# Block 0 by a fixed plan, four loads with places of their own, and tile loads issued from another queue

## The chip, the core and the metric

The kernel runs on one core of a Trainium2 chip. The metric is the device time in microseconds (us) of one execution. A core has five engines with an instruction queue each: TensorE (PE in the profile, with its weight loads as PEld), VectorE (DVE), ScalarE (ACT), GpSimd (POOL) and SyncE (SP). SP computes nothing here; it issues transfers (DMA), which ACT and POOL can do too. Each queue is worked off in order, so an instruction that waits holds up all that stand behind it on its engine.

## The reference

What is computed is an attention without softmax, with a norm, followed by a two-layer network with a leaky relu:

```python
kv = np.einsum('bhsd,bhse->bhde', k, v)          # 8 batches, 8 heads, 576 tokens, 64 wide
out = np.einsum('bhsd,bhde->bhse', q, kv)
rms = np.sqrt(np.mean(out * out, axis=-1, keepdims=True) + 1e-06)
x = (out / rms * g_norm)                          # -> 4608 tokens x 512
h = x @ w_in                                      # 512 x 2048
y = np.maximum(0.01 * h, h) @ w_out               # 2048 x 512
```

q, k, v and g_norm are float32. Both weight matrices arrive as float64 and have to become float32 on the chip.

## The kernel before

The 4608 tokens are nine blocks of 512. A batch has 576 tokens, so block 0 lies in batch 0, and block 1 takes the last 64 tokens of batch 0 and the first 448 of batch 1. For each block the attention makes `xT`, then the network is done chunk by chunk over the 2048 hidden units (four chunks `c` of two halves `h` of two tiles `u` of 128).

The weights are loaded in 32 tiles of 128x512 float64 numbers, 512 KB each; `w_jobs` lists them. A tile of w_in is loaded by four DMA issues, a tile of w_out by one (`load_w`, `load`, L229). A tile lands in one of seven raw places (three in `stage`, four in `pairs`, later two in the tile `early`), and is then rounded by `round_f64`: two activations on ACT (L254, L256), a clamp on DVE (L258), one more activation on ACT (L263), and two DVE instructions (L273 and L276). `round_w` issues the first three steps of one tile and then the rest of the tile before it (`finish_w`), so that a tile's last steps stand behind the first steps of its successor.

`first_attention` loads and works batch 0, and rounds tiles 0 to 4. `first_block` (L1109 on) then computes block 0 with half of the hidden units in plain matmuls: eight hidden tiles n, each a group `h_ps` (x times w_in, needs one tile of w_in), an activation to `g` (L1111), and one step later a group `o_acc` (g times w_out, needs one tile of w_out). Between the groups `between(n, half)` puts in other work: steps of `tail` (the last 64 tokens of batch 0 for block 1), steps of `a_steps` (the attention of batch 1: turning q on DVE at L488, the kv products on PE, then `outputs` and `divide`), and tile loads and roundings. How many of these follow each group is computed from n; the attention's steps stand in a table `steps`.

The loads of batch 1 are four pairs of heads, `load_pair(1, p)`, each with one issue for k, one for v and four for q. They land in tile rings of two, so that pairs 2 and 3 are loaded only when pairs 0 and 1 have been used: the attention's steps issue them.

After that, `product_h`, `product_o` and the code around them do block 1 with all chunks, then the rest of block 0, in Strassen form: seven products of 128x256 groups per chunk in the order 1, 2, 6, 5, 7, 3, 4, in banks named h_a to h_d and o_a, o_c. POOL makes the sums of the weights (`sides_w1` and `sides_w2` into `pairs`), their inner combinations (`combine`), which SP writes to DRAM for the later blocks, and the sums `gs` of the activations (`sums_of`). In these rounds the 15 slots of `W_SLOTS` each round one tile (17 to 31) and load another (up to 31). From block 2 on (about 264 us) the weights are read back in combined form and PE works nearly without a gap.

What sets the order: the framework schedules the instructions of each engine itself, except those that are pinned (`pin`), which keep their written order among one another. Matmuls, roundings and DMA loads are pinned; the activations of `first_block` (all but the last), the squares and copies of `outputs` and `both_outputs`, and the sums on POOL in these stages are not. Transfers issued by SP and ACT take the program's eight DMA semaphores in turn, and each issue waits until the earlier transfer on its semaphore has landed.

The lines that the change touches most:

```python
steps = {2: [tail], 3: [tail], 4: [tail, a_steps], 11: [a_steps, a_steps]}
steps.update((k, [a_steps]) for k in (5, 8, 9, 10, 12, 14))
...
while half and rounded < min(2 * n + 7, n + 10, 4 * K * U + 1):
    load_w(loaded)
    loaded += 1
    round_w(rounded)
    rounded += 1
```

Of the kernel before, what the change touches and what calls it, by code (L numbers as in the profile page):

```python
# [24 lines left out]
def kernel(  # L25
# [36 lines left out]
    nc = tc.nc  # L62
# [27 lines left out]
    ps_m = ctx.enter_context(tc.tile_pool(name="ps_m", bufs=1, space=bass.MemoryType.PSUM))  # L90

    pin = tc.keep_in_program_order
    steady = first_done = in_line = False

    def in_turn(ins):

        if steady or in_line:
            pin(ins)


# [44 lines left out]
            load_pair(b, p, what)  # L145
            n -= 1

    def load_pair(b, p, what="kvq"):


        if "k" in what:
            k_ins[b, p] = load_two(nc.sync, k[b, 2 * p:2 * p + 2], in_tile("k"))
            v_ins[b, p] = load_two(nc.sync, v[b, 2 * p:2 * p + 2], in_tile("v"))
        if "q" not in what:
            return
        t = ins.tile([P, T * D], F32, tag="q_in", name="q_in")
        for l in range(2):
            for c in range(2):
                r0, n = 64 * l + 32 * c, T * D - 32 * c
                src = q[b, 2 * p + half_of(p, l)].rearrange("(t s) d -> t (s d)", s=T)  # L160
                pin(nc.sync.dma_start(t[r0:r0 + 32, :n], src[:, 32 * c:]))
        q_ins[b, p] = t
# [145 lines left out]
    def round_w(j):  # L308
# [4 lines left out]
        finish_w()  # L313
        halfway.append(steps)

    def finish_w():
        while halfway:
            for _ in halfway.popleft():
                pass
# [70 lines left out]
    def outputs(b, lo, hi, e, sums, kv=None):  # L390


        x, n = x_of(lo, hi), hi - lo
        tiles = att_tiles("o_ps")
        o_ps = [t[:, :n] for t in tiles]
        o_products(b, lo, hi, e, o_ps)
        if kv is not None:
            kv_beside(b + 1, kv, tiles)
        for l in range(2):
            sq = t2k(n, "sq" if e else f"sum{l}")  # L400
            nc.scalar.activation(sq, o_ps[l], func=AF.Square)
            if e == 0:
                sums.append(sq)
            else:
                in_turn(nc.vector.tensor_add(sums[l], sums[l], sq))
        for l in range(2):
            nc.scalar.activation(x[:, 2 * l + e, :], o_ps[l], func=AF.Copy, scale=g_sb[:, e:e + 1])

    def divide(lo, hi, sums):

        x, n = x_of(lo, hi), hi - lo
        rms = work.tile([P, 2, n // E], F32, tag="rms", name="rms", bufs=2)
        for l in range(2):
            t = t2k(n, "turned")
            in_turn(nc.vector.transpose(t, sums[l]))
            in_turn(nc.vector.tensor_reduce(rms[:, l, :], t.rearrange("p (a i) -> p a i", i=E),
                                            axis=AX.X, op=ALU.add))
            if l:
                act = nc.scalar.activation(rms, rms, func=AF.Sqrt, scale=1.0 / D, bias=eps_sb)
                if first_done:  # L420
                    pin(act)
            yield
        in_turn(nc.vector.reciprocal(rms, rms))
        spread = []
        for l in range(2):
            t = t2k(n, "spread")
            nc.scalar.copy(t.rearrange("p (a i) -> p a i", i=E),
                           rms[:, l, :].unsqueeze(2).to_broadcast([P, n // E, E]))
            spread.append(t)
        yield  # L430
        for l in range(2):
            inv = t2k(n, "inv")
            in_turn(nc.vector.transpose(inv, spread[l]))
            to = x[:, 2 * l:2 * l + 2, :]
            in_turn(nc.vector.tensor_mul(to, to, inv.unsqueeze(1).to_broadcast([P, 2, n])))
            yield

    def both_outputs(b, lo, hi, sums, kv=None):

        x, n = x_of(lo, hi), hi - lo  # L440
        tiles = att_tiles("o_ps")
        o_ps = [t[:, :2 * n].rearrange("p (e n) -> p e n", e=2) for t in tiles]
        for e in range(2):
            o_products(b, lo, hi, e, [o[:, e, :] for o in o_ps])
        if kv is not None:
            kv_beside(b + 1, kv, tiles)
        for l in range(2):
            sq = t2k(2 * n, "sq").rearrange("p (e n) -> p e n", e=2)
            nc.scalar.activation(sq, o_ps[l], func=AF.Square)
            sums.append(t2k(n, f"sum{l}"))  # L450
            in_turn(nc.vector.tensor_add(sums[l], sq[:, 0, :], sq[:, 1, :]))
        for l in range(2):
            for e in range(2):
                nc.scalar.activation(x[:, 2 * l + e, :], o_ps[l][:, e, :], func=AF.Copy,
                                     scale=g_sb[:, e:e + 1])

    def tail_of(b, lo, hi, fine=False, kv=(None, None)):
        sums = []
# [21 lines left out]
    def attention(b, apart=True, fine=False):  # L480

        qT = qTs[b] = work.tile([P, NP, S], F32, tag="qT", name="qT")
        beside = b > KV_BESIDE
        kv_ps = None if beside else kv_tiles()

        def turn(p):
            q_in = q_ins.pop((b, p))
            in_turn(nc.vector.transpose(  # L488
                qT[:, p, :].rearrange("p (t s) -> p s t", s=T),
                q_in.rearrange("p (s d) -> p s d", d=D)[:, :, :32]))  # L490

        for m in range(2):
            turn(2 * m)
            yield
            turn(2 * m + 1)
            if m:
                yield
            if kv_ps:
                attention_kv(b, m, [t[:, m, :] for t in kv_ps])
            pairs_next = [(b + m, p) for p in ((2, 3) if m == 0 else (0, 1)) if b + m < B]  # L500
            if b == KV_BESIDE and m:
                to_load.extend((b + 1, p, "kv") for p in range(2))
            if apart or m == 0:
                for nxt in pairs_next[:1 if apart else 2]:
                    if apart:
                        to_load.extend((*nxt, what) for what in kinds(b + m))
                    else:
                        load_pair(*nxt)
            yield
            if apart:  # L510
                if m and kv_ps:
                    copy_kv(b, kv_ps)
                for nxt in pairs_next[1:]:
                    to_load.extend((*nxt, what) for what in kinds(b + m))
                yield
        if not apart:
            copy_kv(b, kv_ps)
            yield
        kv = [(None, None), (None, None)]
        if KV_BESIDE <= b < B - 1:  # L520
            kv = [(None, None), (0, 1)] if b > KV_BESIDE else [(None, 0), (None, 1)]
        tails = [tail_of(b, max(i * NT, b * S), min((i + 1) * NT, (b + 1) * S), fine, kv[i - b])
                 for i in (b, b + 1)]
        if not fine:
            for tail in tails:
                yield from tail
            return

        for tail in (0, 0, 0, 0, 0, 1, 0, 0, 1, 1, 1, 1, 1, 1):
            next(tails[tail])  # L530
            yield

    def first_attention():
# [43 lines left out]
        keep_warm(384)  # L577
        for j in range(3, 7):
            load_w(j)
        for p in range(2):  # L580
            load_pair(1, p)
        copy_kv(0, kv_ps)


# [73 lines left out]
        spread(0)  # L658
        for _ in w0:
            pass  # L660
        invert(1)
        spread(1)
        w1 = rounding(1)
# [5 lines left out]
                    next(w1, None)  # L669
        halfway.append(w1)  # L670
        finish_w()
        for j in range(2, 5):
            round_w(j)
        finish_w()


# [416 lines left out]
    def first_block(between):  # L1093
# [3 lines left out]
        for n in range(2 * K * U + 1):  # L1097
            now = last
            if n < 2 * K * U:
# [9 lines left out]
                               stop=(e == NE - 1), skip_group_check=True)  # L1109
                gT = view(g_all[n // 4 % 2], n % 4 * NT, NT)  # L1110
                act = nc.scalar.activation(gT, h_ps, func=AF.Prelu, alpha=SLOPE)  # L1111
                if n == 2 * K * U - 1:
                    pin(act)
                last = (gT, w2_sb[h][c][:, u, :], n)
            if now is None:
                continue
# [11 lines left out]
            nc.scalar.dma_start(part_dram[t * P:(t + 1) * P, :], o)  # L1128

    first_attention()  # L1130
    tail, a_steps = tail_of(0, NT, S), attention(1, False)
    steps = {2: [tail], 3: [tail], 4: [tail, a_steps], 11: [a_steps, a_steps]}
    steps.update((k, [a_steps]) for k in (5, 8, 9, 10, 12, 14))
    loaded, rounded = 7, 5

    def between(n, half):
        nonlocal loaded, rounded
        for each in steps.get(2 * n + half, ()):
            go(each, 1)

        while half and rounded < min(2 * n + 7, n + 10, 4 * K * U + 1):
            load_w(loaded)
            loaded += 1
            round_w(rounded)
            rounded += 1
        if half:
            finish_w()

    first_block(between)
    first_done = True  # L1150
    while loaded < rounded + 5:
        load_w(loaded)
        loaded += 1
    x_sides, _, sums, _ = sides_x(1)
    for _ in sums:
        pass
# [38 lines left out]
    for i, chunks in rounds:  # L1195
# [7 lines left out]
        for c in chunks:  # L1203
# [5 lines left out]
            for t in range(7):  # L1209
# [36 lines left out]
                if one:  # L1246
# [12 lines left out]
                    if at in W_SLOTS:  # L1259
                        round_w(rounded)  # L1260
                        rounded += 1
                        if loaded < len(w_jobs):
                            load_w(loaded)
                            loaded += 1
                    else:
                        finish_w()
# [64 lines left out]
```

## Time and profile before

| what | us |
|---|---|
| median of three runs | 956.05 (955.95 to 956.38) |
| the profiled execution's own time | 955.94 |
| its span, first to last instruction | 954.2 |
| PE busy in the span | 913.7 (96%) |
| block 0, from its first h group to the first group of block 1 | 23.16 to 101.60 |
| block 1's chunk 2, first half | to about 168.7 |

The profile gives the busy time of each engine as a whole and by stretch, a line per group of instructions in order of time, and for each engine what it waited for. A line in order of time has the start, the length, the engine, the source line, the operation, what is written from what, the shape, how many instructions were merged, and in brackets the idle time before them with what ended it. "SPq" and "ACTq" are the issues of transfers; their length contains the waits between merged issues. L numbers are lines of the kernel before unless the changed kernel is spoken of.

### The profile page before, as it was taken

What the parts mean: (1) busy time and instruction counts of PE and PEld (TensorE: products, weight loads), DVE (VectorE), ACT (ScalarE), POOL (GpSimd) and SP (SyncE); (2) the same over time, 40 slices, a digit from 0 to 9 for tenths busy, and PEclk for the clock granted to TensorE, in tenths of its full rate; (3) what the DMA queues carried; (4) which work ended last, traced back from release to release, by engine and by line L of the source; (5) the groups of instructions that cost most, each with busy time, mean ns of one, the idle gap of its engine ahead of it and who ended that gap; (6) DMA issues with size and microseconds to landing.
All of it is one profiled execution on the core that took longest, in us unless ns stands there. A gap on an engine that the chain in (4) does not pass through costs nothing.

```text
span 954.2 us, 18286 instructions
## 1 busy us (share of the span) xinstructions
PE 913.7 (96%) x7072; PEld 797.9 (84%) x7072; DVE 638.1 (67%) x1161; ACT 347.8 (36%) x682; POOL 391.6 (41%) x456
## 2 busy tenths in 40 slices
PE   9996965999999999999999999999999999999998
PEld 5442655788889899989998999999999999999997
DVE  5557774774665687668775877577757765765565
ACT  5535634521323523353335333433344333223331
POOL 2035075588253347224632362226323632462222
PEclk9987988999999999999999999999999999999999
DMA  8991688358968877877788679866965676567632
GB/s 265 222 246 45 224 253 235 117 158 266 313 199 293 277 222 211 266 236 225 224 263 236 223 223 263 239 210 186 258 194 175 183 221 199 180 182 221 200 122 88
DMA packets 92982, 204.26 MB, mean 214 GB/s; under 512 B 10081, under 2 KB 44513, under 8 KB 92897
## 3 DMA queue, kind: packets, MB, share of 16 engines
q1 hardware_dynamic: 81344, 190.19, 67.0%
q10 hardware_dynamic: 11104, 11.73, 3.6%
q8 instruction: 56, 0.92, 0.4%
q0 software_dynamic: 448, 1.18, 0.3%
q14 instruction: 30, 0.24, 0.1%
HBM read 175.54 MB, written 27.53 MB: 213 GB/s over the span
## 4 chain that ended last, share of the span: by engine, by line
PE 78%; DVE 3%; ACT 1%; POOL 1%; issue 1%; DMA 0%; SPq 0%; ACTq 0%; POOLq 0%; DVEq 0%
PE o_a L120 18%; PE o_c L120 17%; PE h_ha L120 10%; PE h_hb L120 10%; PE h_hc L120 8%; PE h_hd L120 8%; PE o_ps L120 2%; PE h_b L120 1%; PE h_a L120 1%; PE h_d L120 1%; PE h_c L120 1%; DVE g L678 1%; PE kv_ps L120 1%; DVE w L273 1%; POOL stage L678 1%
## 5 line engine op out<-in xcount | busy, mean ns | idle before, releaser
L678 POOL TENSOR_TENSOR gs<-g 128x512 f32<-128x512 f32 x68 | 86.9, 1281 | 307.9 <-ACT g L881 307.9
L881 ACT ACTIVATE g<-g 128x512 f32<-128x512 f32 x130 | 82.0, 631 | 147.6 <-DVE g L678 147.6
L1000 ACT COPY w_all<-h_ha 128x512 f32<-128x512 f32 x84 | 49.0, 583 | 171.1 <-PE h_ha L120 165.4
L120 PE MATMUL o_a<-pairs,gs 128*128 128x256 f32 x408 | 97.0, 381 | 0.0
L120 PE MATMUL o_c<-pairs,gs 128*128 128x256 f32 x400 | 94.9, 380 | 0.0
L678 DVE TENSOR_TENSOR o<-o_c,o 128x512 f32<-128x512 f32 (+1 forms) x98 | 66.0, 674 | 32.4 <-PE o_c L120 26.7
L678 DVE TENSOR_TENSOR o<-h_hb,o 128x128 f32<-128x128 f32 x104 | 29.9, 287 | 83.5 <-ACT pairs L1000 82.3
L120 PEld LDWEIGHTS o_a<-pairs,gs 128*128 128x128 f32 x408 | 74.4, 190 | 9.9 <-POOL pairs L678 1.2
L120 PEld LDWEIGHTS o_c<-pairs,gs 128*128 128x128 f32 x400 | 72.9, 190 | 8.3
L678 DVE TENSOR_TENSOR o<-o_a,o 128x512 f32<-128x512 f32 x82 | 56.1, 684 | 32.8 <-PE o_a L120 28.7
L120 PE MATMUL h_ha<-stage,w_all 128*128 128x128 f32 x448 | 59.9, 276 | 0.2 <-POOL stage L678 0.2
L120 PEld LDWEIGHTS h_ha<-stage,w_all 128*128 128x128 f32 x448 | 56.7, 192 | 3.3 <-issue 0.7
L678 DVE TENSOR_TENSOR g<-g,pairs 128x512 f32<-128x512 f32 x84 | 55.7, 689 | 1.9
L678 POOL TENSOR_TENSOR pairs<-g 128x128 f32<-128x128 f32 x52 | 23.7, 456 | 76.2 <-PE h_hb L120 47.5
L678 DVE TENSOR_TENSOR w_all<-h_hc,w_all 128x512 f32<-128x512 f32 x56 | 38.4, 685 | 15.8 <-PE h_hc L120 15.8
L678 DVE TENSOR_TENSOR o<-h_hd,o 128x128 f32<-128x128 f32 x78 | 22.2, 284 | 38.1 <-ACT pairs L1000 38.0
L678 POOL TENSOR_TENSOR gs<-gs,g 128x512 f32<-128x512 f32 x34 | 46.2, 1359 | 2.2
L678 POOL TENSOR_TENSOR gs<-g,gs 128x512 f32<-128x512 f32 x34 | 46.7, 1373 | 0.4
L120 PE MATMUL h_hb<-stage,w_all 128*128 128x128 f32 x336 | 46.7, 275 | 0.0
L1000 ACT COPY pairs<-h_hb 128x384 f32<-128x384 f32 x84 | 40.1, 477 | 13.6 <-PE h_hb L120 12.9
L120 PE MATMUL h_hb<-xT,w_all 128*128 128x128 f32 x224 | 43.3, 275 | 0.0
L120 PE MATMUL h_hd<-xT,w_all 128*128 128x128 f32 x224 | 43.3, 275 | 0.0
(239 smaller groups left out, 2260.2 us busy)
## 6 DMA issues: line engine op xcount, KB each, us to landing
w_all<-w SPq DMA_DIRECT2D x196, 448.0 KB, 4.1
pairs<-w SPq DMA_DIRECT2D x60, 512.0 KB, 4.4
out_dram<-o ACTq DMA_DIRECT2D x35, 256.0 KB, 4.8
v_in<-in_v_dram SPq DMA_DIRECT2D x29, 288.0 KB, 4.5
k_in<-in_k_dram SPq DMA_DIRECT2D x28, 288.0 KB, 4.3
q_in<-in_q_dram SPq DMA_DIRECT2D x56, 144.0 KB, 5.6
q_in<-in_q_dram SPq DMA_DIRECT2D x56, 140.0 KB, 5.7
stage<-in_moe_w_out_dram SPq DMA_DIRECT2D x9, 512.0 KB, 5.5
```

The source lines that it names most:

```text
L120: pin(nc.tensor.matmul(*args, **kw))
L273: pin(nc.vector.scalar_tensor_tensor(dst, in0=cut, scalar=3, in1=dst, op0=ALU.logical_shift_left, op1=ALU.bitwise_or))
L678: ins = eng.tensor_tensor(out_, a, b_, op=ALU.subtract if minus else ALU.add)
L881: nc.scalar.activation(t, t if src is None else src, func=AF.Prelu, alpha=SLOPE)
L1000: nc.scalar.copy(q[:, at], bank)
```

## The change

Block 0 gets a written plan in place of the computed one: which steps of the tail (t), of the attention (a), which rounding (a number) and which finish (f) follow each group. The loads of batch 1's pairs 2 and 3 get places that are free at that time (`homes_1`: the last tiles of the weights, and `early`), and are issued before block 0, in turn with weight tiles 7 to 11. In block 0 the activations of h, and those of the tail and the attention, are pinned to the written order. The tail of batch 0 and the part of batch 1 that lies in block 1 are done in finer steps. In block 1, the tile loads at `W_SLOTS` (tiles 22 to 31) are issued by ACT in place of SP.

```diff
-    steady = first_done = in_line = False
+    steady = first_done = in_line = in_first = False
...
-        if steady or in_line:
+        if steady or in_line or in_first:
+            pin(ins)
+
+    def first_turn(ins):
+
+        if in_first:
             pin(ins)
...
-    def load_pair(b, p, what="kvq"):
+    def load_pair(b, p, what="kvq", homes=None):
...
-            k_ins[b, p] = load_two(nc.sync, k[b, 2 * p:2 * p + 2], in_tile("k"))
-            v_ins[b, p] = load_two(nc.sync, v[b, 2 * p:2 * p + 2], in_tile("v"))
+            for i, (to, src) in enumerate(((k_ins, k), (v_ins, v))):
+                to[b, p] = load_two(nc.sync, src[b, 2 * p:2 * p + 2],
+                                    homes[i] if homes else in_tile("kv"[i]))
...
+    home = view(w1_all, 6 * NW, 2 * NW)
+    w2_last = [w[NC - 1].rearrange("p u n -> p (u n)") for w in w2_sb]
+    n = J * D
+    homes_1 = {2: (view(home, 2 * n, J, D), view(w2_last[0], 0, J, D), view(home, 0, 2 * n)),
+               3: (view(w2_last[1], 0, J, D), view(early, 0, J, D), view(early, n, 2 * n))}
...
-            if apart or m == 0:
+            if apart:
...
-        tails = [tail_of(b, max(i * NT, b * S), min((i + 1) * NT, (b + 1) * S), fine, kv[i - b])
-                 for i in (b, b + 1)]
+        tails = [tail_of(b, max(i * NT, b * S), min((i + 1) * NT, (b + 1) * S),
+                         fine or i == b == 1, kv[i - b]) for i in (b, b + 1)]
...
-        for p in range(2):
-            load_pair(1, p)
+        load_pair(1, 0)
...
+        load_w(7)
+        load_pair(1, 1)
         invert(1)
...
+        load_w(8)
+        load_pair(1, 2, homes=homes_1[2])
         for j in range(2, 5):
             round_w(j)
+            load_w(j + 7)
+            if j == 3:
+                load_pair(1, 3, homes=homes_1[3])
...
-                if n == 2 * K * U - 1:
-                    pin(act)
+                pin(act)
...
+    plan = {(1, 0): (t, 5), (1, 1): (t, t, 6, t), (2, 0): (t, 7, t), (2, 1): (t, f, a),
+            (3, 0): (a, 8), (3, 1): (f, a, 9), (4, 0): (10, f), (4, 1): (11,),
+            (5, 0): (f, a, a, 12, a), (5, 1): (a, 13), (6, 0): (f, a, 14),
+            (6, 1): (a, a, 15, a, f), (7, 0): (a, a), (7, 1): (16,), (8, 0): (f,)}
+    loaded = 12
...
+        for what in plan.get((n, half), ()):
+            if what == f:
+                finish_w()
+            elif what in (t, a):
+                go(tail if what == t else a_steps, 1)
+            else:
+                round_w(what)
+                for j in range(loaded, {12: 17, 13: 18, 14: 19, 15: 20, 16: 21}.get(what, min(what + 7, 16)) + 1):
+                    load_w(j)
+                    loaded += 1
...
-                            load_w(loaded)
+                            load_w(loaded, nc.scalar)
```

## The prediction

> **What bounds the kernel now.** I read first the busy time of each engine by stretch, then what TensorE (PE) waited for, then the instructions of each engine in order of time. From 232 us on PE is the chain and has no idle piece over 1.3 us, so what can move lies before. Busy time by stretch (length, then PE, weight load, DVE, ACT, POOL, clock, DMA share, GB/s): block 0, the first part of block 1, the rest of it.
>
> ```profile
> 23.16:101.60 78.44, 66.62 (x344) 30.46 (x345) 51.93 (x80) 38.02 (x76) 20.92 (x18) 0.89 0.68 159
> 101.60:168.70 67.10, 46.22 (x201) 38.77 (x200) 42.48 (x64) 30.88 (x56) 33.12 (x28) 0.89 0.83 259
> 168.70:232.00 63.30, 62.79 (x441) 53.70 (x442) 43.78 (x67) 18.90 (x38) 45.86 (x39) 0.98 0.54 169
> ```
>
> PE idles 78.44-66.62 = 11.8 us in block 0, 20.9 in block 1's first part. Four waits are nearly all of it (total us, times, longest):
>
> ```profile
> PE h_c L120 <- DVE g L678: 11.5, 1, 11.5
> PE h_ps L120 <- DVE w_all L276: 8.0, 1, 8.0
> PE h_b L120 <- POOL pairs L678: 7.5, 1, 7.5
> PE o_acc L120 <- DVE w L276: 3.8, 1, 3.8
> ```
>
> Their places in PE's order of time (start, us, in brackets the idle time before):
>
> ```profile
> 49.87 6.44 PE L120 MATMUL o_acc<-w,g 128*128 128x512 f32 x8 [3.84 <-DVE w L276]
> 59.58 3.60 PE L120 MATMUL o_acc<-w,g 128*128 128x512 f32 x8
> 80.34 6.58 PE L120 MATMUL h_ps<-xT,w_all 128*128 128x512 f32 x8 [7.98 <-DVE w_all L276]
> 126.77 3.78 PE L120 MATMUL h_b<-xt,pairs 128*128 128x256 f32 x8 [7.50 <-POOL pairs L678]
> 168.70 3.35 PE L120 MATMUL h_c<-xt,pairs 128*128 128x256 f32 x8 [11.50 <-DVE g L678]
> ```
>
> After each, the group runs slow: 6.44 and 6.58 for 3.60, 3.78 and 3.35 for 1.89. Block 0 loses 11.8+5.8 = 17.6 us, the two waits of block 1 19.0+3.4 = 22.4; 40 us is the most that all of this can return.
>
> Who makes them wait, in the order of ACT, SP's queue, POOL:
>
> ```profile
> 46.07 0.60 ACT L1111 ACTIVATE g<-h_ps 128x512 f32<-128x512 f32 x1 [7.67 <-PE h_ps L120]
> 72.48 0.98 ACT L401 ACTIVATE sum<-o_ps 128x448 f32<-128x448 f32 x2 [5.23 <-PE o_ps L120]
> ...
> 85.76 18.88 SPq L229 DMA_DIRECT2D stage<-in_moe_w_in_dram  x4
> ...
> 117.34 2.69 POOL L678 TENSOR_TENSOR gs<-g 128x512 f32<-128x512 f32 x2 [28.22 <-ACT g L881]
> ```
>
> In block 0 ACT stands waiting for PE (an activation of h, a square of o_ps) while roundings (L254 to L276) that PE needs next are queued behind. At 85.76 SP's queue stands 18.9 us: its loads wait, behind one another, for the landing of a write of `part` that ACT issues only after block 0. In block 1 POOL makes the sums gs of chunk 0 first, then the pairs that PE needs (7.5 us); and ACT has the copy of h_a at 155.51 ahead of the rounding of tile 25, so DVE's g add, behind tiles 25 and 26, comes at 167.87 (11.5 us).
>
> **The change, part by part.**
>
> *Loads of batch 1 in homes of their own, interleaved.* The same bytes move. From 24.09 to 65.9 SP issued four pairs (288+288+2x144+2x140 = 1144 KB each) and ten weight tiles (512 KB): 9.9 MB in 41.8 us, 237 GB/s, the DMA engines full. So a pair takes 4.9 us of the stream, a tile 2.2. In the new order: pair (1,0) to 29.0, tile 7 31.2, pair (1,1) 36.2, 8 38.4, pair (1,2) 43.3, 9 45.5, 10 47.7, pair (1,3) 52.7, 11 54.9, 12 57.1, 13 59.3, 14 61.5, 15 63.7, 16 65.9; landing 5 to 7 later (medians of this stretch: 5.3 to 6.6 for tiles). Tile 7 comes 9 us sooner, 8 comes 2 sooner, 9 and 10 are 2 to 4 later, the rest as before. By itself it wins nothing; it feeds the plan.
>
> *The plan of block 0, activations in written order.* No work goes. I laid the built order of the changed kernel out by hand with the rows' durations (start to start): a group of h or o_acc 3.5 us, kv 1.2, o_ps 0.9, a rounding 0.55+0.55 (ACT), 0.35 (DVE), 0.55 (ACT), 0.65+0.65 (DVE). From 34.17 (h 2) PE has 13 groups, two kv, two o_ps: 45.5+2.4+1.8 = 49.7, so 83.9 without a wait. Waits I find: o_acc 2 needs tile 6 at 45.9, done 42.2: none, the 3.8 us is gone. h 5 at 56.4 needs tile 9, whose last steps stand behind the first steps of tile 10 (landing 53 to 54): done 57.0, and 58.7 if POOL's first sums, then released, slow DVE: L273 takes 1.75 us beside POOL at 122.18 and 0.68 without at 151.47. I take 2.3. o_ps of batch 1 needs the turned q of pair (1,3), on DVE behind tile 11 (landing 60 to 61): 1.3. o_acc 5 behind tiles 12 and 13: 0.6. o_acc 6 needs tile 14, whose end stands behind the norm's sums and tile 15: 1.8. Together 6: block 0 ends at 90 in place of 101.6, **11.6 us of the 17.6**. Bounds: 17.6 if loads land 2 us sooner; 5 if they land 4 us later, since 9, 10 and 11 are each needed within 3 us of their landing.
>
> The clock decides whether short waits cost more. The row: idle 3.84 us, then half speed (6.44 for 3.60); idle of 0.86 us at 113.82 leaves 1.99 for 1.89. The Trainium skill ("TensorE: Matmul & The Clock Gate", Part 1) says the clock is halved after an idle window of about 3.4 us. By the rule the 0.6 to 2.3 us waits cost only themselves: end at 90. If each of the three longer ones took the 2.9 us of the long ones, it ends at 98.7. No row here is between 0.9 and 3.8 us; I take the rule, and keep 99 as an end.
>
> *Block 1's tiles issued by ACT.* Ten tiles, 22 issues (six of one, four of four) leave SP's queue. ACT's own such issues took 0.33 us (median of two): 7.3 us more on ACT, which is busy 30.9 of 67.1; hidden there. "DMA: Bandwidth & Descriptors", section "Issuing engines are not separate DMA queues", speaks against it: all issuers share the same DMA engines, and only the sequencer's issue time is saved. By that rule this part is worth nothing on PE's path and costs 7 us of ACT. The rows say otherwise in both directions: SP lost 18.9 us by standing, not by issuing. The built program gives SP's and ACT's issues eight completion semaphores in turn, and each issue waits for the landing of the one before on its semaphore. In front of block 1 tiles 19 and 20 are now free of the `part` writes. But ACT's issues for tiles 24 and 25 now wait for landings of SP's w1 writes, those for POOL's pairs, and behind them in ACT's queue stand the activations of chunk 0 and the copy of h_b that PE waits for.
>
> Counted from the end of block 0 (t = 0; before it was 101.6), landings 4.5 us (medians here 3.6 to 5.3): ACT issues tile 22 at 8.5, lands 13; the SP write behind its semaphore 13 to 17; POOL, which in the new built order makes the pairs of chunk 1 and their combinations before gs, finishes its eighth add at 22; SP's write of them lands at 26 to 27; only then ACT issues tile 25's last piece, makes two operations and copies h_b: 28.4. PE is ready at 18: the wait is **10.5 us where it was 7.5** (+3). Ends: 1 us if only POOL's first two adds count (that wait gone, -6.5), and +8 with landings of 6.7.
>
> The 11.5 us wait goes: tiles 25 and 26 now stand ahead of the copies of chunk 2, the data is there, and DVE's g add needs tile 27's first half only; I get it 1 to 2 us before PE asks. **-11.5, and -1.5** of slow clock. Its other end: it stays, 0. For small waits with so little margin I add 1.5. Block 1: 3-13+1.5 = **-8.5**.
>
> *The finer tails* add pins, no work: 0; their cover is DVE's idle time in block 0 (51.9 busy of 78.4).
>
> Sum: -11.6-8.5 = -20. The span of 954.2 becomes 934, that execution's 955.94 becomes 936; the median of the three runs is 956.05, 0.1 above it, so **936.0**.
>
> **Rivals.** (a) *Tiles late in block 0*: DMA is full there and three margins are under 3 us. For: in five stretches of 12 us from 12 to 72 us the DMA share is 0.86 to 1.08. Against: order and bytes give 237 GB/s already. Block 0 gains 5, total -13: 943. (b) *The long wait in block 1 only moves*: DVE takes tiles 24 to 27 in one stretch of 3.2 us each whenever two scratch pieces alternate. For: that pace stands in the rows at 161 to 170. Against: their data comes earlier. Total -7: 949. (c) *ACT hardly held up*: landings of 2.7 us occur (w2 writes near 170); then the 7.5 us wait shrinks to 1 too and block 0 keeps 15: -15-6.5-13+1.5 = -33, 923. (d) *Slower*: ACT's issues as a chain. Each of the 16 pieces of tiles 24 to 27 may wait a landing, 4.5 us, in one queue with every activation; I count five in the path before h_b. From ten on, 5x4.5 = 22 more, the 20 us are spent; at twelve 31 more: 967. For: the semaphores alternate. Against: by tile 26 most predecessors have landed. (e) *Nothing*: one wait for another, 956.
>
> **How the numbers follow.** Mine 0.55 (929 to 943), a 0.15, b 0.12, c 0.12, d 0.04, e 0.02. A measurement tells about 0.2%, 2 us. Faster: 0.94, same 0.02, slower 0.04. For 8 in 10 the range leaves out d, e, the far side of c and a part of b: 922 to 950.
>
> **What would show it.** Right: no wait over 2.5 us in block 0, its end near 90; the h_c wait on DVE gone; the h_b wait about 10 us with ACT standing at tile loads (L235 of the changed kernel) before it; SP without a stand of 19 us. Wrong: half-speed groups in block 0, a wait of h_ps or o_acc on a rounding of over 4 us; a wait over 5 us in chunk 2; ACT standing in DMA issues more than 20 us together.

## The result and the profile after

The changed kernel took 947.79 us (median of three runs, 946.18 to 948.33) against 956.05 us before: a ratio of 0.9909, with a 95% interval of 0.9887 to 0.9932. It is faster by 8.3 us where the forecast said 20. The range (922 to 950) held the time; the time lies near rival (b), "the long wait in block 1 only moves", 949.

The profiled execution has a span of 946.6 us. Block 0 and the first part of block 1 (to the group for h_c in chunk 2 that waited 11.5 us before), by stretch: length, busy time of PE, weight load, DVE, ACT and POOL with instruction counts, clock, DMA share, GB/s:

```profile
23.00:93.49 70.49, 65.19 (x360) 29.74 (x353) 48.89 (x79) 37.94 (x75) 19.61 (x18) 0.95 0.74 189
93.49:157.02 63.53, 47.50 (x201) 38.90 (x199) 42.94 (x66) 30.23 (x55) 35.15 (x28) 0.92 0.84 271
```

PE's five longest waits, in its order of time (start, us, in brackets the idle time before):

```profile
58.80 5.39 PE L125 MATMUL h_ps<-xT,w_all 128*128 128x512 f32 x8 [2.18 <-DVE w_all L282]
...
77.86 5.40 PE L125 MATMUL o_acc<-w,g 128*128 128x512 f32 x8 [2.56 <-DVE w L282]
...
122.12 3.75 PE L125 MATMUL h_b<-xt,pairs 128*128 128x256 f32 x8 [10.51 <-ACT g L925]
...
157.02 3.04 PE L125 MATMUL h_c<-xt,pairs 128*128 128x256 f32 x8 [2.73 <-DVE g L697]
159.86 2.57 PE L125 MATMUL o_a<-w,g 128*128 128x256 f32 x8
...
171.90 3.45 PE L125 MATMUL h_a<-xt,w_all 128*128 128x256 f32 x8 [2.56 <-DVE g L697]
```

The waits of 3.8 us (o_acc 2), 8.0 us (h) and 11.5 us (h_c) are gone. What is new are five waits of 2 to 11 us, and each of them again has a slow group behind it.

Two lengths carry the rest of this text. Block 0, from its first h group to the first group of block 1: 78.4 us before (23.16 to 101.60), 70.05 after (23.44 to 93.49). Block 1 with the rest of block 0, from there to the first product of block 2: 162.5 before (to 264.06), 163.3 after (to 256.78). So block 0 gave 8.4 us and block 1 took 0.8 back. For each of the other kernels below, these two lengths are read at the same places.

Why PE waits for h_b stands in ACT's queue: it stands at the issues of two tile loads (ACTq), and the copy of h_b comes behind them.

```profile
107.94 4.86 ACTq L235 DMA_DIRECT2D stage<-in_moe_w_in_dram  x4
...
115.26 5.08 ACTq L235 DMA_DIRECT2D stage<-in_moe_w_in_dram  x4
120.39 0.60 ACT L900 ACTIVATE g<-h_a 128x512 f32<-128x512 f32 x1 [5.29 <-DMA stage<-in_moe_w_in_dram]
120.88 0.62 ACT L269 ACTIVATE w<-cut 128x512 int32<-128x512 f32 x1
121.40 0.58 ACT L925 COPY g<-h_b 128x512 f32<-128x512 f32 x1
```

Why it waits in chunk 2 stands in DVE's order of time, here up to the add of h_a that PE waits for at 171.90:

```profile
164.52 1.53 DVE L282 CUSTOM_DVE_ANT_0 w<-w,add 128x1024 uint16<-128x1024 uint16 x1
167.36 0.43 DVE L264 TENSOR_SCALAR cut<-cut 128x512 f32<-128x512 f32 x1 [1.30 <-ACT cut L260]
167.88 1.69 DVE L279 SCALAR_TENSOR_TENSOR w<-cut,w 128x512 uint32<-128x512 uint32 x1
169.49 0.68 DVE L697 TENSOR_TENSOR o<-o_c,o 128x512 f32<-128x512 f32 x1
170.09 1.15 DVE L282 CUSTOM_DVE_ANT_0 w<-w,add 128x1024 uint16<-128x1024 uint16 x1
171.17 0.68 DVE L697 TENSOR_TENSOR g<-h_a,g 128x512 f32<-128x512 f32 x1
```

and in the matching place of ACT:

```profile
166.09 0.68 ACT L262 ACTIVATE add<-stage 128x512 uint32<-128x512 uint32 x1 [3.23 <-DVE w L282]
```

A slot (one of the `W_SLOTS`, in which one tile is rounded) is a round trip between the two engines. ACT's first step of a rounding (L262, 166.09) waits for DVE's last step of an earlier one (L282, ends 166.05), since two scratch pieces are used in turn. DVE's clamp (L264, 167.36) waits for ACT's second step. The finish of the last rounding (L279, L282) stands behind that clamp in DVE's queue, and the add that frees PE's bank behind the finish. DVE idles 1.3 us in the middle. The clamps from 149.45 to 173.64 come 4.8 us apart on average, where PE's two groups of a slot need 3.45. The distance grows with DVE's steps: 3.3 us from 154.37 to 157.66, where POOL was idle (152.5 to 160.7) and L279 and L282 took 0.69 us each; 5.5 and 6.3 us from 161.89 on, where they took up to 1.7 us with POOL at work.

### The profile page after: what moved, and what is told of

It is laid out like the page before. It is cut to its first block, busy times and chain, and to the rows that moved or that the text cites. A ratio compares the mean times of both kernels' runs of the same rounds, so it can differ in the third digit from the quotient of the medians.

```text
span 946.6 us, 18288 instructions
## 1 busy us (share of the span) xinstructions
PE 914.9 (97%) x7072; PEld 798.5 (84%) x7072; DVE 638.6 (67%) x1161; ACT 347.3 (37%) x682; POOL 390.9 (41%) x456
## 4 chain that ended last, share of the span: by engine, by line
PE 84%; DVE 7%; ACT 3%; POOL 2%; DMA 2%; issue 2%; DVEq 0%; ACTq 0%; POOLq 0%; SPq 0%
PE o_a L125 18%; PE o_c L125 17%; PE h_ha L125 10%; PE h_hb L125 10%; PE h_hc L125 8%; PE h_hd L125 8%; PE o_ps L125 3%; PE h_ps L125 2%; PE o_acc L125 1%; DMA w<-w_all 1%; PE h_a L125 1%; PE kv_ps L125 1%; PE h_b L125 1%; DVE w_all L279 1%; DVE w L282 1%
## 5 line engine op out<-in xcount | busy, mean ns | idle before, releaser
L1019 ACT COPY w_all<-h_ha 128x512 f32<-128x512 f32 x84 | 48.9, 582 | 171.8 <-PE h_ha L125 159.8
```

Source lines behind the costliest of these rows:

```text
L1019: nc.scalar.copy(q[:, at], bank)
```

## The experiments

All are edits of the changed kernel unless said otherwise. Each was timed against the kernel before on the same chip; the ratio is to that kernel, with its 95% interval. The forecast, as tested here: part 3 (tile loads of block 1 issued by ScalarE) is worth 8.5 us. Against it: block 1 is paced by its roundings, whoever loads the tiles.

### e1: the third part undone

```diff
-                            load_w(loaded, nc.scalar)
+                            load_w(loaded)
```

> The changed kernel with block 1's tile loads issued by SyncE again (the third part undone). The forecast's step for block 1 (the third part is worth -8.5 us): 956, with the wait for h_b down to about 7.5 us and a wait of about 11 us for h_c back. The theory read off the trace after (block 1 gained nothing, because the roundings of its second half set the pace whatever engine issues the loads): 947, within 1.5 us of the changed kernel's 947.8, block 1 again some 162.5 us from the end of block 0 to the first product of block 2.

Measured 947.59 us, 0.9917 (0.9897 to 0.9937): the same as the changed kernel. Block 1 took 162.65 us. PE in order of time:

```profile
113.64 1.97 PE L125 MATMUL h_b<-xt,pairs 128*128 128x256 f32 x8 [0.26 <-POOL w_all L697]
...
159.64 3.75 PE L125 MATMUL h_c<-xt,pairs 128*128 128x256 f32 x8 [10.89 <-DVE g L697]
```

With block 0 changed, the wait for h_b is as good as gone (0.26 us; before it was 7.5), and the wait for h_c stands at 10.9. Three more waits, of 2.3 to 2.9 us, stand ahead of an h_a, an h_d and an h_b, where the changed kernel has its two of chunk 2. The third part trades the one set for the other and wins nothing.

### e2: the third part alone, in the kernel before

```diff
-                            load_w(loaded)
+                            load_w(loaded, nc.scalar)
```

> The kernel before with the third part alone: block 1's tile loads issued by ScalarE. The forecast's step: 956.05 - 8.5 = 947.5. The theory that the roundings' pace takes it back: 956 to 957; block 0 unchanged, the wait for h_b some 3 us longer, the 11.5-us wait for h_c in pieces of 0.7 to 3 us, each longer one followed by a group at a slower clock.

Measured 964.38 us, 1.0073 (1.0045 to 1.0101): slower, which neither expectation had. Block 1 took 171.9 us, 9.4 more than before:

```profile
132.20 3.75 PE L120 MATMUL h_b<-xt,pairs 128*128 128x256 f32 x8 [11.63 <-ACT g L906]
...
148.50 3.66 PE L120 MATMUL h_b<-xT,pairs 128*128 128x256 f32 x8 [6.15 <-ACT g L913]
```

In ACT's queue, the longest of its four stands at tile loads (5.4, 4.3, 9.7 and 1.9 us):

```profile
134.26 9.73 ACTq L229 DMA_DIRECT2D stage<-in_moe_w_in_dram  x4
```

PE waits for two copies of h_b by ACT, 17.8 us together, and the waits of 2.7 and 2.6 us in chunk 2 are there too. This is the mechanism of rival (d), ACT's issues as a chain, with the old block 0 in front.

### e3: extra matmuls in block 0's two waits

Two matmuls of 0.9 us into a bank that the next group overwrites, ahead of h 5 and of o_acc 5.

```diff
+                if n == 5:
+                    warm(h_ps, x, 2)
...
+            if n == 6:
+                h_next.append(ps_m.tile([P, NT], F32, tag="hc", name="h_ps"))
+                warm(h_next[0], x, 2)
```

> The changed kernel with two extra matmuls (0.9 us each, into a bank that the next group overwrites; the output stays the reference's) ahead of h 5 and two ahead of o_acc 5, where TensorE stood 2.18 and 2.56 us. Theory that the idle time itself slows the clock: both groups go back from 5.4 to about 3.6 us, block 0 ends 3.6 us sooner (89.9 instead of 93.49) and, if block 1 follows, 944.2. Rival, that these groups are slow for another reason (operands, transfers beside them): they stay at 5.4 us and the time at 947.8, or up to 0.5 more if the extra matmuls reach past the waits. Second rival: block 0 ends sooner and block 1 gives it back, since its roundings were late anyway: 947 to 948 with the end of block 0 at 90.

Measured 946.76 us, 0.9908 (0.9889 to 0.9927).

```profile
58.74 3.70 PE L125 MATMUL h_ps<-xT,w_all 128*128 128x512 f32 x8 [0.57 <-DVE w_all L282]
...
76.38 3.70 PE L125 MATMUL o_acc<-w,g 128*128 128x512 f32 x8 [0.67 <-DVE w L282]
...
85.04 7.11 PE L125 MATMUL o_acc<-w,g 128*128 128x512 f32 x16 [1.53 <-DVE w L282]
```

Both groups are back at 3.7 us, as in e8 and e15, which have the same extra matmuls; so the idle time had slowed them. But block 0 is only 1.2 us shorter (68.8 for 70.05), not 3.6: a wait of 1.53 us ahead of o_acc 6 is new, for a rounding that was ready no earlier. One of the two slow groups had been free. The time cannot be told from the changed kernel's; the profiled spans differ by 1.9 us (944.7 and 946.6).

### e4: the clamp behind the finish of the last rounding

```diff
-        for _ in range(3):
+        for _ in range(2 if first_done else 3):
             next(steps, None)
         finish_w()
+        if first_done:
+            next(steps, None)
```

> The changed kernel with one reordering after block 0: a rounding's clamp on VectorE stands behind the finish of the rounding before it, not ahead of it. Two scratch pairs are in turn, so ScalarE's first step of the next rounding waits for that finish; with the clamp ahead, the finish waits for ScalarE's two steps of the rounding in between. Theory that this round trip paces block 1's second half: the cycle of at least 3.2 us falls below TensorE's 3.45 us for two groups, the waits of that half (0.7, 2.7, 2.6 us) and the slow groups behind them (together 9.6 us) fall to 3 or less: about 942. Rival, that VectorE slowed by GpSimd (1.6 instead of 0.7 us for a step) or the arrival of the tiles paces it: 947 to 948.

Measured 948.90 us, 0.9932 (0.9908 to 0.9955); block 1 took 166.2 us in the profiled execution, which at 952.19 us was the slowest of four. No gain, and the edit was the wrong one: the finish begins with a step on ACT (L269), which still stood behind ACT's two steps of the next rounding, so the round trip had stayed:

```profile
156.94 0.69 ACT L262 ACTIVATE add<-early 128x512 uint32<-128x512 uint32 x1 [2.26 <-DVE w_all L282]
157.53 0.65 ACT L260 ACTIVATE cut<-early 128x512 f32<-128x512 f32 x1
158.36 0.63 ACT L269 ACTIVATE w_all<-cut 128x512 int32<-128x512 f32 x1 [0.18 <-DVE cut L264]
```

### e5: the pairs loaded ahead of the tiles

```diff
-        load_w(7)
         load_pair(1, 1)
+        load_pair(1, 2, homes=homes_1[2])
+        load_pair(1, 3, homes=homes_1[3])
+        load_w(7)
```

and the two later `load_pair` calls taken away.

> The changed kernel with the loads of batch 1's pairs 1, 2 and 3 put ahead of the loads of tiles 7 to 11, as far as the order of before, but with their new places and the new plan kept. The forecast's step (the 3.8-us wait ahead of o_acc 2 goes because tile 7's load comes ahead of the pairs): that wait is back, 3 to 4 us with a group at a slower clock behind it, and block 0 ends 4 to 5.5 us later: 952 to 953. Rival, that the plan alone (the places of the roundings) took the wait away and the pairs' own places let SyncE pass quickly: no such wait and 947 to 948.

Measured 961.47 us, 1.0053 (1.0036 to 1.0069): slower than the kernel before. On PE and on ACT:

```profile
57.25 6.07 PE L125 MATMUL o_acc<-w,g 128*128 128x512 f32 x8 [11.30 <-DVE w L282]
```

```profile
53.92 0.66 ACT L262 ACTIVATE add<-stage 128x512 uint32<-128x512 uint32 x1 [15.14 <-DMA stage<-in_moe_w_in_dram]
```

o_acc 2 needs tile 6, whose last steps stand behind the first steps of tile 7; tile 7 lands late, and with it all waits: 11.3 us and the slow group, where I expected 4 to 5.5. But the edit goes further than the order of before. There SP issued tiles 7 to 10 (from 35.92 us on) ahead of pairs 2 and 3 (from 44.32); here tile 7 is issued at 46.95, behind all pairs. So e5 shows that the new plan needs its tiles early: the order of the loads decides whether block 0 gains 8 us or loses 6. It does not show that the old order of the loads made the 3.8-us wait of the kernel before.

### e6 and e7: the finish first, with loads by ScalarE and by SyncE

```diff
         steps = rounding(j)
+        if first_done:
+            finish_w()
         for _ in range(3):
             next(steps, None)
         finish_w()
```

e7 has the edit of e1 as well.

> The changed kernel with one reordering after block 0: in each slot the finish of the last rounding (a step on ScalarE, two on VectorE) stands ahead of the first steps of the next one. The clamp moved alone (e4) left the same round trip, since the finish's step on ScalarE still stood behind the two steps of the next rounding. Theory that the round trip ScalarE - VectorE - ScalarE in each slot paces block 1's second half: the waits for h_c and h_a (2.7 and 2.6 us) and the slow groups behind them go to a third or less, 942 to 944. Rival, that VectorE's work itself, slowed beside GpSimd, paces it: 947 to 948. The wait for h_b (10.5 us) stays in both.

> The same reordering with block 1's tile loads issued by SyncE, as in e1. In e1 the wait for h_b was 0.3 us and the wait for h_c 10.9 us, with three roundings in a row between the last product and that wait. Theory of the round trip: the 10.9 us fall to some 5 or less: 940 to 942. Rival, that VectorE's work, or the order of the roundings among the products, sets that wait whatever the order within a slot: 946 to 948.

e6 measured 941.37 us, 0.9845 (0.9831 to 0.9860). PE, and DVE in chunk 2:

```profile
120.79 3.75 PE L125 MATMUL h_b<-xt,pairs 128*128 128x256 f32 x8 [10.75 <-ACT g L927]
...
155.59 1.99 PE L125 MATMUL h_c<-xt,pairs 128*128 128x256 f32 x8 [0.52 <-DVE g L699]
```

```profile
161.10 0.41 DVE L264 TENSOR_SCALAR cut<-cut 128x512 f32<-128x512 f32 x1
161.44 0.68 DVE L699 TENSOR_TENSOR o<-o_a,o 128x512 f32<-128x512 f32 x1
162.21 0.99 DVE L279 SCALAR_TENSOR_TENSOR w<-cut,w 128x512 uint32<-128x512 uint32 x1
163.24 0.69 DVE L282 CUSTOM_DVE_ANT_0 w<-w,add 128x1024 uint16<-128x1024 uint16 x1
163.85 0.42 DVE L264 TENSOR_SCALAR cut<-cut 128x512 f32<-128x512 f32 x1
```

DVE's holes are gone, the clamps come 3.5 us apart (150.94 to 168.38), and the 2.7- and 2.6-us waits are 0.5 and none; three others of 0.6 to 1.3 us are there in chunk 2, with no slow group behind them. Block 1 took 158.9 us, 4.4 less than in the changed kernel. Another 1.6 us of this execution's gain are block 0's, 68.4 for 70.05 us, where no line was changed: in this execution neither of its two short waits slowed the clock. e7 measured 943.37 us, 0.9866 (0.9850 to 0.9882); its h_c wait fell from 10.9 to 6.8, block 1 took 159.8. The round trip did pace chunk 2. DVE's work beside POOL, the rival, did not do so by itself: in the 32 us from 143 on POOL was busy 21.3 us in e6 and 17.0 in the changed kernel, and five of the eight last steps of a rounding (L282) still took 1.6 us in e6.

### e8: e7 with the matmuls of e3

> e7 with the extra matmuls of e3 in block 0. e3 ended block 0 1.5 us sooner. If block 1 follows: 1.5 us less than e7; if block 1's roundings are bound to something that began in block 0, the same as e7.

Measured 943.00 us, 0.9863 (0.9846 to 0.9879): not to be told from e7, though its profiled block 0 was 2.4 us shorter (68.46 and 70.83).

### e9: the finish first in the kernel before

> The kernel before with the reordering of e6 alone (the finish of the last rounding ahead of the first steps of the next, after block 0). If the round trip within a slot made the 11.5-us wait for h_c in before too: that wait falls to 5 to 7 us and the time to 950 to 952. If that wait was of late tiles or of SyncE's queue, as the forecast had it in part: it stays, 955 to 957.

Measured 954.34 us, 0.9980 (0.9972 to 0.9988). The 11.5-us wait fell to 7.19, but a wait of 2.49 came ahead of an earlier h_b: 1.9 us in all, where I expected 4 to 6. So about 4 of the 11.5 us were the round trip in the kernel before too.

### e10 and e11: the roundings one slot sooner

```diff
-    W_SLOTS = (1, 2, 4, 5, 7, 8, 10, 11, 12, 13, 14, 15, 16, 17, 18)
+    W_SLOTS = (1, 2, 4, 5, 7, 8, 9, 10, 11, 12, 13, 14, 15, 16, 17)
```

on e6 (e10) and on e7 (e11).

> e6 with block 1's roundings of slots 10 to 18 each one slot sooner (slot 9 was left without one). If block 1 is still short of roundings where it waits: its waits of its second half (0.6, 1.3, 1.0, 0.5 us) fall, 939 to 940. If PE is held by something else by then: 941, and if the denser order delays the copies and adds that stand behind it: 942 to 944.

> e7 (tile loads by SyncE, finish first) with the roundings of slots 10 to 18 one slot sooner. e7 waits 6.8 us for h_c with a slow group behind. If that wait is the roundings standing in a row ahead of one add on VectorE, a slot of 3.45 us more of lead takes half of it: 938 to 940. If the tiles come too late from SyncE for that: 943 to 945, with ScalarE or VectorE waiting for the transfers.

e10 measured 944.91 us, 0.9873 (0.9847 to 0.9899), e11 951.92 us, 0.9955 (0.9945 to 0.9965): e11 is slower than e7, and slower than either theory had it; e10's interval overlaps that of e6 (0.9831 to 0.9860), so it is not shown to be slower. In e11 the h_c wait stayed at 6.8 and a wait of 3.73 us for a group of h_b, on DVE, came ahead of it. A rounding put sooner also stands sooner ahead of the adds that PE needs. Only argued: no run separates this from the earlier loads that go with it.

### e12, e13, e14: single tiles back on SyncE

```diff
-load_w(loaded, nc.scalar)
+load_w(loaded, nc.sync if loaded in (24, 25) else nc.scalar)
```

e12 is this on e6, e14 on the changed kernel itself; e13 is e6 with tiles 24 to 27 on SyncE.

> e6 with tiles 24 and 25 alone issued by SyncE (the two for which ScalarE stood 4.9 and 5.1 us in front of the copy of h_b), all others by ScalarE. If those stands are the price of the third part: the wait for h_b falls from 10.7 to 3 us or less, and if nothing else takes its place 934 to 936. If block 1 is paced by its roundings as a whole, a wait for h_c comes back in its place: 940 to 943.

> e12 with tiles 26 and 27 issued by SyncE as well; in e12 ScalarE still stood 2.2 and 2.4 us at them, and TensorE waited 2.7 and 5.0 us for h_d. If these waits come from those stands: they go, 933 to 935. If SyncE then brings the tiles late, or the roundings in a row ahead of the wait for h_c set it, as in e7: 939 to 943.

> The changed kernel with tiles 24 and 25 alone issued by SyncE and the order within a slot as it was. If ScalarE's stands cost by themselves: the wait for h_b goes from 10.5 to 3 us or less and the time to 942 to 945. If the round trip of the roundings takes it back: a longer wait for h_c or h_a comes in its place, 946 to 948, as in e1.

e12: 938.36 us, 0.9818 (0.9799 to 0.9838). e13: 943.15 us, 0.9862 (0.9847 to 0.9876). e14: 944.60 us, 0.9873 (0.9858 to 0.9888). PE in e12:

```profile
112.57 1.97 PE L125 MATMUL h_b<-xt,pairs 128*128 128x256 f32 x8 [0.95 <-ACT g L927]
...
131.31 3.61 PE L125 MATMUL h_d<-xT,pairs 128*128 128x256 f32 x8 [4.96 <-ACT g L929]
...
152.63 1.99 PE L125 MATMUL h_c<-xt,pairs 128*128 128x256 f32 x8 [1.82 <-DVE g L699]
```

and SP's queue and PE in e13:

```profile
120.93 14.26 SPq L235 DMA_DIRECT2D stage<-in_moe_w_in_dram  x4
```

```profile
154.81 3.75 PE L125 MATMUL h_c<-xt,pairs 128*128 128x256 f32 x8 [5.87 <-DVE g L699]
```

The h_b wait was ACT's two stands: without them it is 0.95 us. Only a part of those 10 us comes through: 3.0 us of block 1 with the old order in a slot (e14), 5.0 with the new (e12). The median times fell by 3.2 and 3.0, for the profiled e12 has a slow group in block 0 that e6 has not. e12 lies between the two expectations: waits of 2.7 and 5.0 us ahead of h_d came in place of the one for h_b. With four tiles on SyncE its queue stands 14 us and the h_c wait is back. Block 1's length, all nine together:

| us, block 1 | all by ACT | 24, 25 by SP | 24 to 27 by SP | all by SP |
|---|---|---|---|---|
| block 0 of before, old slot | 171.9 (e2) | | | 162.5 (before) |
| block 0 changed, old slot | 163.3 (after) | 160.3 (e14) | | 162.7 (e1) |
| block 0 changed, finish first | 158.9 (e6) | 153.9 (e12) | 160.0 (e13) | 159.8 (e7) |

### e15: e12 with the matmuls of e3

> e12 with the extra matmuls of e3 ahead of h 5 and o_acc 5. Block 0 of e12 ended at 93.0 with one slow group. If block 1 follows the end of block 0: 1.5 us less than e12, 937. If not: 938.4.

Measured 936.66 us, 0.9789 (0.9773 to 0.9806), the fastest of all, 11 us less than the changed kernel. The step from e12 (1.7 us) is within the two intervals; the rest is the order in a slot and the two tiles.

## Why the forecast was half right

**Block 0's plan and loads: right in kind, 11.6 us forecast, 8.4 measured.** No wait over 4 us is left; the three waits (2.18, 0.55 and 2.56 us; 5.3 together) come to the 6 that was forecast, at the places it named but for o_acc 6. That the sums agree is in part luck: o_acc 5 was put at 0.6 us and waited 2.56, o_acc 6 at 1.8 and did not wait. The wait ahead of o_acc 2 is gone as forecast. In the kernel before, tile 6's end stood behind tile 7's first steps; tile 7 had landed at 43.4, but ACT began it only at 46.57, behind an activation of h for which it had stood 7.67 us (the row at 46.07). Now tile 7 lands at 36.3, and ACT begins it at 38.86, ahead of that activation (44.95). So by the traces it was mostly the order on ACT that made this wait; no run tests the order alone, and e5 shows only that the plan needs its tiles early.

**The step that failed here is the clock.** "By the rule the 0.6 to 2.3 us waits cost only themselves." They cost 1.8 us each on top. No wait in blocks 0 and 1 of the kernel before lay between 0.9 and 3.8 us, and I read the figure of about 3.4 us in the Trainium skill ("TensorE: Matmul & The Clock Gate", Part 1) as a threshold for one wait. The same part says that the window runs free and that results vary with its phase, and the traces bear that out. In each of the 17 profiled executions all changes of the granted clock lie on one grid of 3.41 us (until the program's end, half speed lasts 3.41, 6.83, 10.24 or 13.65 us at a time), and how the grid lies to the program differs. What counts is how long PE is busy within a window of that grid. Here are the two windows around h 5 in the changed kernel, then in e6 (stretch, its length, PE busy; third from the end is the clock):

```profile
55.42:58.83 3.41, 1.23 (x4) 0.22 (x2) 3.31 (x3) 0.63 (x2) 3.25 (x3) 1.00 1.06 267
58.83:62.24 3.41, 3.41 (x4) 1.47 (x5) 3.02 (x3) 1.23 (x2) 3.33 (x4) 0.50 1.11 236
...
54.49:57.91 3.42, 1.68 (x4) 0.38 (x2) 3.27 (x3) 1.60 (x3) 3.19 (x3) 1.00 1.07 268
57.91:61.32 3.41, 2.98 (x7) 1.44 (x8) 3.38 (x4) 0.75 (x2) 3.33 (x4) 1.00 1.10 238
```

The same wait of 2.18 us lies in one window in the first and over a border in the second. From 24 to 930 us, over all 17 traces, each of the 61 full-speed windows in which PE was busy 44% or less was followed by one at half speed, and none of the 4345 with 46% or more. So a wait of 2 to 3 us can cost more than itself, and whether it does depends on where it falls on a grid that the program does not set: luck, as far as the forecast goes. The 11 kernels of this case with the new block 0 and no extra matmuls wait 2.2 to 2.3 us ahead of h 5 and 2.56 to 2.58 ahead of o_acc 5; the group behind took 5.2 to 5.4 us in 9 of 11 and in 4 of 11, and 3.6 to 3.7 in the others. Waits of 0.45 to 1.31 us at the same places (e3, e8, e15) slowed none of six. Yet the clock is only 1.6 us of the 3.2 missing here: block 0 took 68.4 us in e6, where no group was slow, since o_acc 6 then waits 1.5 us for its tile. The other 1.6 us are waits (6.9 together in e6, not 6) and groups some 0.1 us longer after each break.

**ACT's issues ahead of h_b: right.** 10.5 us forecast, 10.51 measured; the copy 28.4 us after block 0's end forecast, and PE's group began 28.6 after it. e12 shows the cause. What I had not seen is the other side: without the third part that wait would not have been 7.5 but 0.3 us (e1), for the changed kernel had already removed it in another way: POOL makes these pairs before the sums gs, from 103.38 us in e1 and 106.13 in the changed kernel, where it came to them at 123.34 before. The forecast names this new order, yet took the 7.5 over from the profile before.

**"The 11.5 us wait goes ... -11.5, and -1.5 of slow clock", with 1.5 added for small waits: this step failed, and it is most of the error.** The wait went, but chunk 2 then lost 9.6 us in pieces: 0.7, 2.7 and 2.6 us of waits, 3.4 us of slow groups (3.04, 2.57 and 3.45 for 1.89), and 0.2 at a later group. The term of 1.5 should have been 9.6; about 1.2 more is small change around h_b (a wait of 0.59, a group of 2.60 for 2.00). So block 1 came to +3.0+1.2-13.0+9.6 = +0.8 and not -8.5. The pace that the forecast names, 3.2 us a rounding, was read off roundings whose steps on DVE ran undisturbed (0.69 us at 163 to 168); the same round trip took 4.8 us on average where some of these steps took 1.5 to 1.7 us, with POOL busy at the same time. The forecast had reckoned with such steps in block 0 (1.75 for 0.68 us) and left them out here. Rival (b) named it, at 12 in 100, and "a wait over 5 us in chunk 2" as its sign was too coarse: it came as several of 2.7. e6 shows the round trip as the cause: one reordering and chunk 2's two longer waits are 0.5 us and none. Late tiles were not the limit there: with all of them on SyncE again (e1), no instruction of ACT or DVE waits for a landing between 125 and 172 us.

**SP free of the `part` write: wrong, and without effect.** Its queue still stood 10.6 us at 84.46 for tiles 19 and 20, 9.8 of them for that landing, and no wait of PE leads back to it.

What stays open: why the third part costs 9.4 us of block 1 behind the old block 0 (e2) and 0.6 behind the new one (after against e1); what makes the 6.8 us of waiting for h_c that remain in e7, where roundings still stand in a row ahead of the add; and what e11 loses by.

## What to carry to other kernels

Before a wait is struck from a sum, ask what paces the stretch behind it: a two-piece scratch between two in-order queues is a round trip per step, and writing the finish of one step ahead of the start of the next was worth more here than any choice of queue for the loads. An issue that waits for a semaphore holds up all that stands behind it in the issuer's queue, so put loads on an engine whose next instructions nobody waits for, tile by tile if need be. Where an earlier part of a change moves a stage, work its later waits out anew rather than take them from the profile before.

## What the runs showed of the hardware

The clock granted to TensorE changes on a fixed grid of 3.41 us. In these traces a window of it in which TensorE was idle for 1.92 us or more was followed by one at half speed, and one with 1.85 us or less was not; half speed then lasted until a window was 82% busy (none of 48 with 78% or less ended it). So idle time of 2.2 to 2.6 us halved the clock of the group behind it in 13 of 22 cases, with 5.2 to 5.4 us for a group of 3.6. The extra matmuls that fill such a wait took the slow groups away in all six cases (idle time left: 0.45 to 1.31 us).
